# Unread products of zeros in TensorE's planned waits, and batch 1's V loads, spreads and casts behind batch 0's

## The chip, the core and the metric

The kernel runs on one core of one Trainium2 chip. The core has five engines with a queue each, which run side by side and wait for one another by semaphores: TensorE (PE; matrix products into PSUM), VectorE (DVE), ScalarE (ACT), GpSimd (POOL) and SyncE (SP). The queues of SP, ACT and POOL issue DMAs, which 16 DMA engines carry out. The instructions of each engine are brought from HBM by DMA as well. The metric is the device time of one execution in microseconds; lower is better.

## The reference

Two stages, one behind the other: attention with local and global tokens, then a hard-swish MLP over all tokens.

```python
k_all = np.concatenate([k_g, k_l], axis=2)
v_all = np.concatenate([v_g, v_l], axis=2)
out_g = np.matmul(sm(scale * q_g @ k_all.T), v_all)
mask = np.abs(pos[:, None] - pos[None, :]) <= 32
s_ll = np.where(mask, scale * q_l @ k_l.T, -1e9)
out_l = np.matmul(sm(np.concatenate([scale * q_l @ k_g.T, s_ll], -1)), v_all)
x = concat([out_g, out_l], axis=2) as tokens x 512
h = x @ w_in
out = (h * np.clip(h + 3.0, 0.0, 6.0) / 6.0) @ w_out
```

8 batches, 8 heads of 64, 512 local and 32 global tokens a batch, w_in 512 x 2048, w_out 2048 x 512. In the kernel products run in 16 bit with sums in 32 bit.

## The kernel before

Tokens of a batch are cut into 16 blocks of 32 queries; each sees 128 keys: its own block, the block on each side and the 32 global ones. Two blocks from each half of the sequence are a *pair* in what follows: `local` (L697) runs four of them a batch, with 64 score products of TensorE (L731 for batches 0 and 1, L718 for later ones), eight maxima of VectorE (L762), eight exponentials of ScalarE (L768), eight transposes of TensorE (L777), a copy out of PSUM (`et`, L319/L321), 32 products with V (L795), a division (L804, L805) and a transpose into the MLP's layout (L818). Batch 0's pairs run in the order 1, 0, 2, 3; the text counts them first to fourth. `globe` (L822) does the global queries in two halves. The MLP's first product is L926, with ScalarE's relu (L937) and VectorE's gate (L933) behind it; the second is L953. Batch 0's MLP starts pair by pair, with 128 columns for the first two pairs and 256 for the last two.

V is needed in a layout in which the keys of one block stand in the 128 partitions (`vs`). SP's DMAs spread the global rows into it (L532), and copies of *strips* from `v0` (L561) do the rest, on GpSimd for later batches and on any of three engines in batch 0. K and q are turned by VectorE transposes (L609, L614), and at the halves' edges small copies (`halo`, L631) complete K.

The order of all this isn't written by hand. Every operation is put into a named stream with a rank (L297), with its engine or engines, a planned duration and its dependencies. `Plan.lay` (L123) takes, again and again, the operation that can start first by its own clock, and among those that can start within 0.03 us on the same engine the one of lowest rank. It emits them in that order, and the hardware runs each engine's instructions in it. `holds` and a dependency that is added to a plan operation bind the order that is planned. The planner has its own idea of TensorE's instruction supply: blocks of `BLOCK` = 256 instructions, each usable `FETCH` after the edge before it was crossed (`stalls`, L113), and of a slow TensorE (`SLOW`) before `COLD`. None of this appears in the program itself.

At the start TensorE gets a *pad* (L1015): 100 products of a 32x32 tile of zeros with two columns, which nobody reads.

Lines that matter below: `g_first` and `once` load batch 0's and 1's global q and k rows and cast them (L461, L486), `v_loads` (L536) issues V's loads and the strips, `vg_load` and `spread` (L517, L526) the global rows of V, `load_w_in` and `load_w_out` the weights.

Of the kernel before, what the change touches and what calls it, by code (L numbers as in the profile page):

```python
# [9 lines left out]
FP32 = mybir.dt.float32  # L10
# [27 lines left out]
class Plan:  # L38
# [2 lines left out]

    LANES = 8
    BLOCK = 256
    FETCH = 3.4
    COLD, SLOW = 30.0, 1.9
    SWITCH, ALONE = 0.097, 0.0
    SPARE, PHASES = 0.4, 9

    def __init__(self, pools, claims):
        self.count, self.fetched, self.mode = 60, 0.0, "full"  # L50
        self.claims = claims
        self.tune = TUNE
        self.issued = {}
        self.free = {p: [0.0] * n for p, n in pools.items()}
        self.streams = {}
        self.rank = {}
# [66 lines left out]
    def lay(self):  # L123
        at = self.at = {n: 0 for n in self.streams}
        clock = {}
        order = []
        total = sum(len(s) for s in self.streams.values())
        while len(order) < total:
# [43 lines left out]
            at[n] += 1  # L172
            if op.landing is not None:
                self.issued.setdefault(e, []).append(op.landing)
            if e == "PE":
                wait, when = self.stalls(op, start, self.cost(op, e, start))
                end += wait
                self.mode = op.mode[1]
                if self.count % self.BLOCK + op.n >= self.BLOCK:
                    self.fetched = when + wait + self.FETCH + min(3.0, max(0.0, clock.get("DMA", 0.0) - when - 0.5))  # L180
                self.count += op.n
            clock[e] = end
            op.end, op.engine = end + op.lat, e
# [10 lines left out]
def kernel(  # L194
# [52 lines left out]
    def tiles(name, n, shape, dtype, pool=None):  # L247
        return [(pool or sb).tile(shape, dtype, tag=f"{name}{i}", name=f"{name}{i}") for i in range(n)]
# [88 lines left out]
    def quarter(e, f):  # L337
        return slice((2 * e + f) * W, (2 * e + f + 1) * W)
# [121 lines left out]

    def g_first(b):  # L461

        after = [w_in_l[1][1]] if b else []
        state[b]["gl"] = {}
        for k, src, name in ((1, k_g, "k"), (0, q_g, "q")):
            if b == 0:
                once(k, src, name)
                continue
            rows = src[b].rearrange("(c e) g d -> e g c d", e=2)
            g, w, got = Buf("gn" + name, 1), Buf("gr" + name, 1), []  # L470
            state[b]["gn", k] = g
            for e in range(2):
                for f in range(2):
                    got.append(load("sh" if b else "ga" if k else "g0", "SP" if b or not k else "ACT", 0.47, 0.2, graw[k][quarter(e, f)], rows[e], after, () if got else [w]))

            def cast(engine, k=k):
                o, i = (t[k].rearrange("p c d -> p (c d)") for t in (gn0, graw))
                if engine == "ACT":
                    nc.scalar.copy(out=o, in_=i)
                else:  # L480
                    nc.vector.tensor_copy(out=o, in_=i)
            op = Op({"ACT": 0.37, "DVE": 0.3}, None, got, [g], [w])
            op.emit = lambda op=op, cast=cast: cast(op.engine)
            state[b]["gl"][k] = [plan.add("gc", op)]

    def once(k, src, name):  # L486

        raw_ = ots[k][0:W].rearrange("g (h d) -> g h d", d=D)
        got = load("ga", "ACT", 0.47, 0.3, raw_, src[0].rearrange("h g d -> g h d"))
        state[0]["gn", k] = Buf("gn" + name, 1)  # L490
        state[0]["gl"][k] = []
        for e in range(2):
            for f in range(2):
                def cast(engine, e=e, f=f):
                    o, i = gn0[k][quarter(e, f)], raw_.rearrange("g (c e) d -> g e c d", e=2)[:, e]
                    if engine == "ACT":
                        nc.scalar.copy(out=o, in_=i)
                    else:
                        nc.vector.tensor_copy(out=o, in_=i)
                op = Op({"ACT": 0.37, "DVE": 0.3} if k else {"ACT": 0.37}, None, [got], [state[0]["gn", k]] if not state[0]["gl"][k] else [])  # L500
                op.emit = lambda op=op, cast=cast: cast(op.engine)
                state[0]["gl"][k].append(plan.add("gc" if k else "gd", op))

    def g_rest(b0, to):

# [20 lines left out]
    def spread(b, units_, after):  # L526

        st = state[b]
        v = st["v"]
        for u in units_:  # L530
            a = ORDER[u].index("g") * W
            st["vs"][u, 0] = [load("sh", "SP", 0.5, 0.3, lambda u=u, a=a: vs[v.slot][a:a + W, u],  # L532
                                lambda: vg[v.slot][0:W].rearrange("p (j h) d -> p j h d", j=1).to_broadcast([W, NJ, H, D1]), [after], lat=2.0 + LATE[b])]
            st["vs"][u, 1] = list(st["vs"][u, 0])

    def v_loads(b, to):  # L536
# [6 lines left out]
        vl = [load(to, "POOL", 0.8, 1.05 if b else 1.25, lambda j=j: v0[v.slot][:, j, :, 0:D],  # L543
                   v_l[b, :, j * P:(j + 1) * P, :].rearrange("h s d -> s h d"), lat=LATE[b] if b else 3.3 - 0.4 * j) for j in range(NJ)]
# [467 lines left out]

    with tc.manual_schedule():
        clean = plan.add("first", Op(("DVE", 0.1), lambda: nc.vector.memset(zero, 0.0)))
        plan.add("pad", Op(("PE", 4.0), lambda: [nc.tensor.matmul(out=aps[0][0:W, 0, 0:2], lhsT=zero, rhs=zero[:, 0:2], start=True, stop=True) for _ in range(100)], [clean],  # L1015
                           n=200, mode=("small", "small")))
# [79 lines left out]
```

## Time and profile before

| | us |
|---|---|
| median of 3 runs (330.26 to 330.88) | 330.26 |
| the profiled execution | 331.21 |
| its span, first to last instruction | 329.4 |
| TensorE busy, of the span | 306.1 (93%) |
| VectorE busy | 259.6 (79%) |
| ScalarE busy | 236.7 (72%) |
| GpSimd busy | 154.7 (47%) |

The profile shows one execution. "Busy" is the time in which an engine executes; an instruction that waits isn't busy. A line of a wait names who waited, then who ended the wait ("issue": nothing that the profile shows), the total, how often and the longest. A line in order of time has start and length in us, the engine, the line of the kernel, the operation, output and inputs by the program's names, shape and count, and in brackets the idle time before it. PEld is TensorE's weight load. PEclk is TensorE's clock as granted, as a share of full speed; where there is no record yet, it is shown as full.

The largest groups of TensorE are L953 (560 products, 131.8 us) and L926 (640, 121.6 us); of VectorE L933 (136, 92.0 us) and L762 (56.2 us); of GpSimd L561 (87 strips, 79.4 us).

### The profile page before, as it was taken

To read this page: it belongs to the slowest core of one execution; us is meant where nothing else is said; L and a number is where in the kernel's file an instruction comes from. 1 tells how busy PE (TensorE), PEld (TensorE's weight loads), DVE (VectorE), ACT (ScalarE), POOL (GpSimd) and SP (SyncE) were. 2 spreads that over 40 slices of the span, in tenths; PEclk is the share of its full clock that TensorE was granted. 3 is DMA by queue.
4 is the path that set the end of the run, shared out by engine and by line. 5 is a ranking of instruction groups with operands and counts; after the bars stand their busy time and mean duration, and the time that the engine had idled before them with its cause. 6 is when DMAs were issued, how large, how long until landed. Compare 5 with 4: busy or idle time off the path is not lost.

```text
span 329.4 us, 11223 instructions
## 1 busy us (share of the span) xinstructions
PE 306.1 (93%) x4484; PEld 172.8 (52%) x4484; DVE 259.6 (79%) x916; ACT 236.7 (72%) x545; POOL 154.7 (47%) x201
## 2 busy tenths in 40 slices
PE   4457889999989999999999999999999999999995
PEld 3336786555545555555554554554455545556653
DVE  7789996898878898989899899898898874672210
ACT  7869668757977798769867987589758796553221
POOL 9998299409995802993249519923800000000000
PEclk9977999999999999999999999999999999999999
DMA  8999999999952996299969991998211012101222
GB/s 199 186 207 193 206 210 113 176 251 162 191 106 66 157 178 124 47 134 180 211 88 147 169 131 34 120 190 145 62 39 34 2 34 67 32 2 33 65 57 72
DMA packets 105429, 39.67 MB, mean 120 GB/s; under 512 B 92256, under 2 KB 98144, under 8 KB 105376
## 3 DMA queue, kind: packets, MB, share of 16 engines
q0 software_dynamic: 91392, 16.91, 65.8%
q1 hardware_dynamic: 13440, 21.91, 28.2%
q8 instruction: 35, 0.57, 0.7%
q10 hardware_dynamic: 544, 0.13, 0.2%
q14 instruction: 18, 0.15, 0.1%
HBM read 35.26 MB, written 8.91 MB: 134 GB/s over the span
## 4 chain that ended last, share of the span: by engine, by line
PE 76%; POOL 9%; issue 6%; DVE 4%; ACT 2%; DMA 1%; SPq 0%; POOLq 0%
PE m L953 32%; PE m L926 31%; PE t L777 3%; POOL vs L561 3%; PE a L795 3%; PE s L718 2%; POOL v L309 2%; DMA rawq<-rawq 1%; PE s L835 1%; PE t L866 1%; PE a L876 1%; DVE gts L933 1%; PE s L731 1%; DVE x L805 1%; PE m L731 1%
## 5 line engine op out<-in xcount | busy, mean ns | idle before, releaser
L953 PE MATMUL m<-wout,gts 128*128 128x512 f16 (+1 forms) x560 | 131.8, 373 | 0.0
L926 PE MATMUL m<-xt,win 128*128 128x512 f16 (+2 forms) x640 | 121.6, 339 | 3.3 <-DVE gts L933 3.3
L933 DVE SCALAR_TENSOR_TENSOR gts<-t,m 128x512 f16<-128x512 f32 x136 | 92.0, 681 | 30.5 <-ACT t L937 29.0
L937 ACT ACTIVATE t<-m 128x512 f32<-128x512 f32 x136 | 80.8, 596 | 43.4 <-PE m L926 41.2
L561 POOL COPY vs<-v 32x1056 f32<-32x1056 f32 (+5 forms) x87 | 79.4, 912 | 48.9 <-DMA v<-in_v_l_dram 44.8
L926 PEld LDWEIGHTS <-win 128*128 128x128 f16 x704 | 70.7, 114 | 49.6 <-issue 4.9
L768 ACT ACTIVATE ex<-sm,mx 128x128 f16<-128x128 f32 x256 | 86.3, 395 | 10.1 <-DVE mx L762 9.5
L953 PEld LDWEIGHTS <-gts 128*128 128x128 f16 x560 | 51.2, 98 | 49.8 <-issue 2.4
L762 DVE CUSTOM_DVE_ANT_0 sm<-s,mask 128x128 f32<-128x128 f32 x240 | 56.2, 284 | 8.1 <-PE s L731 3.2
L961 ACT COPY ot<-m 128x512 f32<-128x512 f32 (+1 forms) x35 | 20.0, 572 | 12.6 <-PE m L953 12.6
L319 ACT COPY et<-t 128x1024 f16<-128x1024 f16 x26 | 26.2, 1006 | 3.3 <-PE t L777 3.1
L309 POOL DMA_DIRECT2D v<-in_v_l_dram x32 | 28.2, 900 | 0.0
L309 POOL DMA_DIRECT2D rawq<-in_q_l_dram x12 | 12.6, 1056 | 23.9 <-DVE qt L665 13.0
L805 DVE TENSOR_TENSOR x<-a,rec 128x512 f16<-128x512 f32 x32 | 22.1, 692 | 1.1
L818 DVE STREAM_TRANSPOSE xt<-x 128x512 f16<-128x512 f16 x32 | 22.4, 701 | 0.2
L762 DVE DVE_READ_ACCUMULATOR2_ANT mx<- 128x1 f32 x256 | 21.2, 83 | 0.0
L777 PEld LDWEIGHTS <-ex 128*128 128x128 f16 x256 | 17.4, 102 | 6.3 <-issue 0.4
L777 PE MATMUL t<-ident,ex 128*128 128x128 f16 x240 | 19.2, 225 | 0.0
L795 PEld LDWEIGHTS <-et 128*32 128x32 f16 x1024 | 10.0, 97 | 14.1 <-ACT ex L768 3.8
L665 DVE STREAM_TRANSPOSE qt<-rawq 128x512 f16<-128x512 f16 x24 | 15.8, 687 | 0.6 <-DMA rawq<-rawq 0.6
L795 PE MATMUL a<-vs,et 128*32 128x65 f16 x1024 | 14.2, 196 | 2.0 <-ACT et L319 1.1
L319 ACT COPY etg<-t 128x640 f16<-128x640 f16 x15 | 10.4, 693 | 7.6 <-PE t L866 7.5
(93 smaller groups left out, 220.4 us busy)
## 6 DMA issues: line engine op xcount, KB each, us to landing
out_dram<-ot SPq DMA_DIRECT2D x62, 128.0 KB, 2.4
vs<-vg SPq DMA_DIRECT2D x32, 132.0 KB, 7.6
v<-in_v_l_dram POOLq DMA_DIRECT2D x32, 128.0 KB, 9.1
rawq<-in_q_l_dram POOLq DMA_DIRECT2D x12, 256.0 KB, 5.8
rawk<-in_k_l_dram POOLq DMA_DIRECT2D x12, 256.0 KB, 7.6
rawq<-rawq SPq DMA_DIRECT2D x12, 254.0 KB, 7.1
rawk<-rawk SPq DMA_DIRECT2D x12, 254.0 KB, 7.5
win<-in_moe_w_in_dram POOLq DMA_DIRECT2D x4, 512.0 KB, 10.3
```

The lines of the kernel that those rows point to most:

```text
L309: eng.dma_start(out=o() if callable(o) else o, in_=i() if callable(i) else i)
L319: nc.scalar.copy(out=o(), in_=i())
L561: (nc.gpsimd if op.engine == "POOL" else nc.vector).tensor_copy(out=o(), in_=i())
L762: nc.vector.tensor_tensor_reduce(out=sms[sm.slot], in0=scored(c // 2)[:, z:z + P], in1=mask(m), scale=-scale, scalar=3.0e38, op0=ALU.add, ...
L768: nc.scalar.activation(out=exs[ex.slot][:, un, c, :], in_=sms[sm.slot], func=EXP, scale=-1.0, bias=mxs[mx.slot])
L777: nc.tensor.matmul(out=turned(tp)[:, z:z + P], lhsT=exs[ex.slot][:, un, c, :], rhs=ident, is_transpose=True)
L795: nc.tensor.matmul(out=o[hq * W:(hq + 1) * W, 4 * f + 2 * un + kh, 0:D + 1], lhsT=ets[et.slot][:, un, c, quarter(e, f) if b >= WORDS else ...
L805: nc.vector.tensor_tensor(out=xs[x.slot].rearrange("p g (a d) -> p g a d", a=2), in0=o[:, :, 0:D].rearrange("p g (d a) -> p g a d", a=2), ...
L926: nc.tensor.matmul(out=mps[ps.slot][:, k * n:(k + 1) * n], lhsT=column_tile(c)[:, m], rhs=x, start=(m == 0), stop=(m == KC - 1))
L933: nc.vector.scalar_tensor_tensor(out=g, in0=shape(t1s[t1.slot][:, 0:all_]), scalar=1.0, in1=shape(mps[ps.slot][:, 0:all_]), op0=ALU.min, o ...
L937: r = plan.add("t1", Op(("ACT", 0.09 + all_ * 0.00083), lambda: nc.scalar.activation(out=t1s[t1.slot][:, 0:all_], in_=mps[ps.slot][:, 0:al ...
L953: nc.tensor.matmul(out=mps[ps.slot][:, 0:n], lhsT=gfn(c), rhs=w_out_t[c // 4][:, c % 4, cols], start=(c == 0), stop=(c == NDFF - 1))
```

## The change

The planner's numbers change: `COLD` 30 to 16 us, `SPARE` 0.4 to 0.8 (what an operation that could also run on ScalarE must save to be put on VectorE), the supply of instructions 7.0 us a block before 40 us and 5.2 after, and many ranks. Wherever the planner's own TensorE clock has a gap of over 0.4 us between 6 and 60 us, it now puts in products of zeros with zeros, which fill 65% of the gap at a planned 0.057 us each. They write 62 columns at the end of a PSUM tile in which the products with V leave these columns unused. 40 of the pad's 100 products become such full products. Batch 1's global rows are loaded once, in two DMAs rather than eight, and cast by eight smaller copies on ScalarE or GpSimd. In the plan's order, batch 1's global V load on GpSimd comes behind batch 0's last strip, and batch 1's spreads behind the third load of w_out.

```diff
-    FETCH = 3.4
-    COLD, SLOW = 30.0, 1.9
-    SWITCH, ALONE = 0.097, 0.0
-    SPARE, PHASES = 0.4, 9
+    COLD, SLOW = 16.0, 1.9
+    SWITCH, ALONE = 0.097, 0.5
+    GAP, SHARE, FILL = 0.4, 0.65, (6.0, 60.0)
+    SPARE, PHASES = 0.8, 9
...
+            gap = start - clock.get("PE", 0.0)
+            if e == "PE" and self.fill and self.GAP < gap and self.FILL[0] < start < self.FILL[1]:
+                n = int(self.SHARE * gap / 0.057)
+                filler = Op(("PE", gap), lambda n=n: self.fill(n), n=2 * n)
+                filler.end, filler.engine = start, "PE"
+                order.append((clock["PE"], "fill", filler))
+                total += 1
+                self.count += filler.n
+                self.mode = "full"
...
-                    self.fetched = when + wait + self.FETCH + min(3.0, max(0.0, clock.get("DMA", 0.0) - when - 0.5))
+                    self.fetched = when + wait + (7.0 if when < 40.0 else 5.2)
...
-    graw = tiles("graw", 2, [P, NC, D], FP32)
+    graw0 = tiles("graw0_", 1, [W, 2, H, D], FP32)[0]
...
-    zero = tiles("zero", 1, [W, W], FP16)[0]
+    zero = tiles("zero", 1, [P, P], FP16)[0]
...
-    for name, rank in (("l0", 0), ("ld", 5), ("lq", -2), ("sh", 0), ("sq", 0), ("st", 2), ("g0", 0), ("ga", -9), ("first", -9), ("pad", -30), ("gc", -6), ("gd", 3), ("cast", -5), ("msk", lambda n: 1 if n < 9 else 1.25), ("tq", lambda n: 0 if n < 8 else 3), ("kg", -1), ("vs", 2.2), ("clr", 1),
-                       ("s", 0.5), ("mx", lambda n: 1.2 if n < 33 else 2.7), ("ex", 1.2), ("t", -0.5), ("etc", 0), ("av", -0.7), ("nm", 1.5),
-                       ("xp", -0.5), ("gx", 1),
-                       ("mf", lambda n: 9 + n * 1e-3), ("ms", lambda n: 9 + (n + len(PARTS) * NDFF + 2) * 1e-3), ("t1", 0), ("gate", -0.7), ("ot", 0)):
+    for name, rank in (("l0", 0), ("ld", 5), ("lq", -2), ("sh", 0), ("sq", 0), ("st", 2), ("g0", 0), ("ga", -9), ("first", -9), ("pad", -30), ("gc", -6), ("gd", 3), ("gp", 3.9), ("cast", -5), ("msk", lambda n: 1 if n < 9 else 1.25), ("tq", lambda n: 1.5 if n < 8 else 4.5), ("kg", 0.5), ("vs", 2.2), ("clr", 1),
+                       ("s", 0.5), ("mx", lambda n: 1.2 if n < 33 else 2.7), ("ex", 0.5), ("t", 1), ("etc", 0), ("av", -0.7), ("nm", 0),
...
+    def once(b, k, src, name):
+        raw_ = (graw0[:, k] if b else ots[k][0:W].rearrange("g (h d) -> g h d", d=D))
+        got = load("sh" if b else "ga", "SP" if b else "ACT", 0.47, 0.45 if b else 0.3, raw_, src[b].rearrange("h g d -> g h d"), [w_in_l[1][1]] if b else ())
...
+                op = Op({"POOL": 0.43, "ACT": 0.42} if b else {"ACT": 0.42, "DVE": 0.4} if k else {"ACT": 0.42}, None, [got], [] if e or f else [g])
...
-            op = Op({"POOL": c, "ACT": c, "DVE": c if n == W else 1.35 * c} if b == 0 else {"POOL": c}, None, [vl[j + dj] for j in js])
+            op = Op({"POOL": 0.25 + 0.205 * len(js), "ACT": 0.2 + 0.22 * len(js), "DVE": c if n == W else 1.35 * c} if b == 0 else {"POOL": c}, None, [vl[j + dj] for j in js])
...
+        def unread(n):
+            for _ in range(n):
+                nc.tensor.matmul(out=aps[0][:, 1, 512 - 62:], lhsT=zero, rhs=zero[:, 0:62], start=True, stop=True)
+        def pad():
+            for _ in range(60):
+                nc.tensor.matmul(out=aps[0][0:W, 1, 512 - 62:512 - 60], lhsT=zero[0:W, 0:W], rhs=zero[0:W, 0:2], start=True, stop=True)
+            unread(40)
+        plan.add("pad", Op(("PE", 3.3), pad, [clean], n=200, mode=("small", "full")))
+        plan.fill = unread
...
+        for u in range(NU):
+            state[1]["vs"][u, 0][0].deps[0].deps.append(w_out_l[NDFF // 2])
...
+        state[1]["g4"].deps[0].holds = {"POOL": made["strips"][-1][1]}
```

In the order that is built, TensorE has 4,625 products rather than 4,484, each with its weight load.

More of the change, by code (lines that the diff above doesn't have):

```diff
@@ L52, in __init__ @@
         self.tune = TUNE
-        self.issued = {}
+        self.issued, self.fill = {}, None
         self.free = {p: [0.0] * n for p, n in pools.items()}
@@ L296 @@
     plan = Plan(sizes, {})
[L297 to L300 removed]
+    for name, rank in (("l0", 0), ("ld", 5), ("lq", -2), ("sh", 0), ("sq", 0), ("st", 2), ("g0", 0), ("ga", -9), ("first", -9), ("pad", -30), ("gc", -6), ("gd", 3), ("gp", 3.9), ("cast", -5), ("msk", lambda n: 1 if n < 9 else 1.25), ("tq", lambda n: 1.5 if n < 8 else 4.5), ("kg", 0.5), ("vs", 2.2), ("clr", 1),
+                       ("s", 0.5), ("mx", lambda n: 1.2 if n < 33 else 2.7), ("ex", 0.5), ("t", 1), ("etc", 0), ("av", -0.7), ("nm", 0),
+                       ("xp", 1), ("gx", 1),
+                       ("mf", lambda n: 9 + n * 1e-3), ("ms", lambda n: 9 + (n + len(PARTS) * NDFF + 2) * 1e-3), ("t1", 0), ("gate", -1.4), ("ot", 0)):
         plan.stream(name, rank)
@@ L461, in g_first @@
     def g_first(b):
-        after = [w_in_l[1][1]] if b else []
         state[b]["gl"] = {}
         for k, src, name in ((1, k_g, "k"), (0, q_g, "q")):
[L466 to L491, printed above, removed]
+            once(b, k, src, name)
+    def once(b, k, src, name):
+        raw_ = (graw0[:, k] if b else ots[k][0:W].rearrange("g (h d) -> g h d", d=D))
+        got = load("sh" if b else "ga", "SP" if b else "ACT", 0.47, 0.45 if b else 0.3, raw_, src[b].rearrange("h g d -> g h d"), [w_in_l[1][1]] if b else ())
+        g = Buf("gn" + name, 1)
+        state[b]["gn", k] = g
+        state[b]["gl"][k] = []
         for e in range(2):
@@ L498, in cast @@
                     else:
-                        nc.vector.tensor_copy(out=o, in_=i)
-                op = Op({"ACT": 0.37, "DVE": 0.3} if k else {"ACT": 0.37}, None, [got], [state[0]["gn", k]] if not state[0]["gl"][k] else [])
+                        (nc.gpsimd if engine == "POOL" else nc.vector).tensor_copy(out=o, in_=i)
+                op = Op({"POOL": 0.43, "ACT": 0.42} if b else {"ACT": 0.42, "DVE": 0.4} if k else {"ACT": 0.42}, None, [got], [] if e or f else [g])
                 op.emit = lambda op=op, cast=cast: cast(op.engine)
-                state[0]["gl"][k].append(plan.add("gc" if k else "gd", op))
+                state[b]["gl"][k].append(plan.add("gp" if b else "gc" if k else "gd", op))
     def g_rest(b0, to):
@@ L531, in spread @@
             a = ORDER[u].index("g") * W
-            st["vs"][u, 0] = [load("sh", "SP", 0.5, 0.3, lambda u=u, a=a: vs[v.slot][a:a + W, u],
+            st["vs"][u, 0] = [load("sh", "SP", 0.5, 0.45, lambda u=u, a=a: vs[v.slot][a:a + W, u],
                                 lambda: vg[v.slot][0:W].rearrange("p (j h) d -> p j h d", j=1).to_broadcast([W, NJ, H, D1]), [after], lat=2.0 + LATE[b])]
@@ L542, in v_loads @@
             made["ident"] = plan.add("clr", Op(("POOL", 0.55), lambda: make_identity(nc, ident)))
-        vl = [load(to, "POOL", 0.8, 1.05 if b else 1.25, lambda j=j: v0[v.slot][:, j, :, 0:D],
+        vl = [load(to, "POOL", 0.88, 1.05 if b else 1.25, lambda j=j: v0[v.slot][:, j, :, 0:D],
                    v_l[b, :, j * P:(j + 1) * P, :].rearrange("h s d -> s h d"), lat=LATE[b] if b else 3.3 - 0.4 * j) for j in range(NJ)]
@@ L1014 @@
         clean = plan.add("first", Op(("DVE", 0.1), lambda: nc.vector.memset(zero, 0.0)))
-        plan.add("pad", Op(("PE", 4.0), lambda: [nc.tensor.matmul(out=aps[0][0:W, 0, 0:2], lhsT=zero, rhs=zero[:, 0:2], start=True, stop=True) for _ in range(100)], [clean],
-                           n=200, mode=("small", "small")))
+        def unread(n):
[7 more added lines that the diff above has]
+        plan.fill = unread
         plan.add("first", Op(("DVE", 3.4), setup))
```

## The prediction, on record before the result was known

> **What bounds the kernel now.** I read the 40 slices first, then TensorE's waits in the first 60 us, then the order of time around the longest of them. The slices:
>
> ```profile
> PE   4457889999989999999999999999999999999995
> DVE  7789996898878898989899899898898874672210
> PEclk9977999999999999999999999999999999999999
> DMA  8999999999952996299969991998211012101222
> ```
>
> A slice is 8.2 us. From the sixth on TensorE is full, so the end is set by when that state is reached and by the work that is left then. After 60 us it idles 0.8, 0.6 and, at the end, 4.0 us (20.00 less 19.16, 40.00 less 39.44, 29.40 less 25.36 in the busy times by stretch). The rest of its 23.2 us of idle time (329.4 less 306.15), some 17.8, is in the start. TensorE's waits from 0 to 60 us (total, times, longest):
>
> ```profile
> PE s L731 <- DVE kt L624: 3.6, 1, 3.6
> PE m L731 <- issue: 3.5, 1, 3.5
> PE s L731 <- DVE kt L614: 3.3, 2, 2.5
> PE m L926 <- DVE gts L933: 3.3, 3, 1.6
> PE m L731 <- POOL kt L631: 1.6, 1, 1.6
> ```
>
> Four name a producer. The 3.5 us of "issue" has none. In order of time, TensorE and then VectorE:
>
> ```profile
> 18.55 0.35 PE L731 MATMUL m<-kt,qt 32*32 32x128 f16 x19
> 22.39 0.83 PE L731 MATMUL m<-kt,qt 32*32 32x128 f16 x45 [3.50 <-issue]
> 23.15 1.03 PE L777 MATMUL m<-ident,ex 128*128 128x128 f16 x8
> 50.72 0.61 PE L777 MATMUL t<-ident,ex 128*128 128x128 f16 x8
> ```
>
> ```profile
> 21.13 0.69 DVE L805 TENSOR_TENSOR x<-a,rec 128x512 f16<-128x512 f32 x1
> 23.33 0.29 DVE L762 CUSTOM_DVE_ANT_0 sm<-m,mask 128x128 f32<-128x128 f32 x1 [1.51 <-PE m L731]
> ```
>
> TensorE stops inside one group of 64 equal products, so no operand is missing: its instructions are. The page's queue table says what brings them:
>
> ```profile
> q8 instruction: 35, 0.57, 0.7%
> ```
>
> 35 packets of 16 KB for a stream of 8,988 instructions are 64 B each, 256 to a packet. At the stop 706 had been issued; with 62 of a preamble that is 768, the third edge of 256. The packets' starts in the trace fit this: 5.43, 20.12, 26.33, 33.08, 39.16 us, behind the first edges' crossings at 3.5, 15.6, 22.4, 28.6 and 35.4 by 1.9, 4.5, 3.9, 4.4 and 3.8. So crossing one edge asks for the block behind the next one. The block that stopped TensorE was asked for at 15.6, came from 20.12 to 21.12 and was usable at 22.39: 6.8 us. With the lags of 3.8 to 4.5, 1.0 for the packet and 1.3 until use, a block takes 6.1 to 6.8 us while the DMA engines are full. In that time TensorE gets 128 products, whatever they are.
>
> The stop costs VectorE only the 1.51 us shown, for it had work queued. VectorE then carries the start (busy, in stretches, behind the arrow of each row's PE and PEld):
>
> ```profile
> 21.33:28.15 6.82, 5.26 (x123) 4.24 (x123) 5.11 (x24) 4.28 (x12) 6.64 (x10) 0.50 1.17 202
> 28.15:42.16 14.01, 10.30 (x256) 8.92 (x254) 13.62 (x25) 10.12 (x22) 5.81 (x11) 1.00 1.48 202
> 42.16:60.00 17.84, 17.58 (x396) 12.91 (x395) 14.11 (x73) 14.57 (x39) 17.35 (x20) 1.00 1.53 162
> ```
>
> 13.62 of 14.01 us is VectorE; from 42.16 TensorE has 17.58 of 17.84. The first row also has the clock at 0.50. The eight transposes took 1.03 us there and 0.61 at full clock.
>
> **The change part by part.** *The unread products.* 100 stand in the pad as before, 40 of them now full tiles; 141 more stand in ten groups: 13, 24, 23, 10, 5, 7, 5, 14, 24 and 16. Their form is not in the trace. From below the pad's 28 ns (2.82 us over 100), from above the 111 ns of a half-clock 128x128 product (1.77 us over 16 at 26.68). I take 62/128 of the latter, 53 ns, as they stream 62 columns; 141 are 7.5 us (3.9 to 15.7). In time they are mostly covered: the 24 and 23 lie in the idle stretches before 10.50 and 11.88 (2.53 and 0.77 us in the trace), 24 behind the third pair's values under ScalarE's exponentials, the last 16 under VectorE's 2.06 us of L614 transposes. Three groups first wait until VectorE has read the same PSUM tile (L805 twice, L893 once); behind them queue the second pair's transposes, the fourth pair's (their exponentials come later still) and products that need a gate behind L614. Without that cover the 24 would cost 1.3 us.
>
> *What they should bring.* Full clock from early on is worth half of TensorE's cold work on the chain: transposes 0.4 us a pair, scores 0.3 (64 in about 1.0 us at 16.8, 0.7 at 44.4), so up to 1.5 us for pairs one and two, and nothing where VectorE is the bound. I take 0.5.
>
> By the Trainium skill (TensorE: Matmul & The Clock Gate, Part 1) a busy window of about 3.4 us gives full clock and one idle window takes it away. The trace agrees: 1.00 granted for 3.4 us from 17.91, 0.50 for 6.8, then 1.00. By it alone the whole 1.5 us would be kept.
>
> *What they take.* 282 instructions are 1.1 blocks, and they come where blocks are scarce. The built order puts the edges so. The second falls on the last of the first pair's third set of scores, which waits for L614 at about 12.7 us (12.3 in the trace; two maxima now stand before it, two times 0.21). The third falls on the 41st of 64 scores of the third pair; those can start near 16.6 (15.87 plus 1.0 in the trace). Its block is usable at 12.7 plus 6.1 to 6.8, 18.8 to 19.5, where before all 64 scores, the first values and 19 products more were done by 18.9. The fourth falls inside the five unread products just ahead of the second pair's transposes. Between the two edges TensorE has 23 scores, 7 unread, 32 values, 64 scores: about 2 us. It then waits to 19.2 plus 6.1 to 6.8, 25.3 to 26.0, and the transposes start at 25.8, against 23.15. Evacuation 1.0 us (24.22 in the trace, 1.01), values 0.5 and the division 0.9 put x of the second pair's end at 28.7 to 29.6, against 27.57. Fifth edge, inside the third pair's values: 31.4 to 32.8, against 28.4 for these values.
>
> From there the fourth pair's chain (transposes, 1.0 us of copy, 20 MoE products, values, 0.9 of division) ends at 37 to 38.4, against 33.8. VectorE comes to batch 1's L609 at 38.1 to 39.7, against 35.02: 3.1 to 4.7 late, with one gate (0.66) and its product group (1.0 us of TensorE) more behind it. Subtracting the 1.0, TensorE is full 2.1 to 3.7 us later.
>
> *VectorE's share.* Two maxima before L614 rather than behind it, a copy etg (0.45) and two strips (0.43, 0.74) to ScalarE or GpSimd: 1.6 us less for VectorE, of which I count 0.5, since in the new order it waits, not TensorE for it. Bound 0 to 1.6.
>
> *Batch 1's V, spreads and casts.* GpSimd takes four strip copies (0.65 each, 2.65 us for four at 21.15) ahead of V's loads, which then go out at about 28 rather than 24.5; behind them w_out's. The values of batch 1 run at 57.9, the loads landed at 37.6, so 3 to 4 us is covered. Without cover it would be 3.5. SP issues two loads of batch 1's global rows rather than eight, ahead of the four spreads in either kernel; nothing there waits. Eight casts of 32x256 (0.40 each, ScalarE five, GpSimd three) replace two of 0.41: 1.2 us more on ScalarE, in its 1.53 us of waiting at 37.
>
> *The ranks* move instructions of all batches, but the groups of TensorE's modes stay as they are (67 returns to full tiles before, 68 after), and TensorE is full: 0, between minus 1.0 and plus 1.0 (the 1.4 us of idle time, or as much again).
>
> **Sum** against the profiled execution, 331.21 us (span 329.4 and 1.8 around it): plus 2.9 (mid of 2.1 to 3.7), minus 0.5 and 0.5 gives plus 1.9, 333.1. The runs' median is 0.95 lower: 332.2.
>
> **Rivals.** *The blocks come in time.* The first lag was 1.9 us, with few small packets under way. With it a block takes 4.2 us; the third edge would be served at 16.9, the fourth at 21.1, just as they are reached. Then the 3.5 us are gone: the second pair's exponentials are done near 20, transposes, copy, values and division (0.5, 1.0, 0.5, 0.9, and some queueing on ScalarE) put its x at 24.3, VectorE's 7.9 us of work from there to L609 at 32.2 rather than 35.0, and the end at 330.26 less 2.8, 327.5. For it: the DMA engines' later lag of 2.4 at 43.1. Against: four of the five lags from 15 to 36 us are near 4, and the engines are full until 54.
>
> The Trainium skill (Runtime: NRT & Kernel Launch, Instruction fetch mechanics) has blocks of 256 instructions with crossings "mostly hidden"; by that this rival holds. The block size agrees with the trace, the 3.50 us stop does not.
>
> *The clock falls in the wait before the fourth edge.* 4 us without products, then half clock: transposes and MoE products of pairs two to four take 1.5 to 2 us more on the chain: 334.0. For it: after 18.90 to 22.39 the clock was 0.50 for 6.8 us. Against: part of it lies under VectorE.
>
> *It comes to nothing:* the stalls eat just the gain of clock and order, 330.3.
>
> **How the numbers follow.** Two stalls as forecast 0.48 (own range 331.0 to 333.6), blocks in time 0.28 (327.0 to 329.5), clock falling as well 0.16, nothing 0.08. Within 0.2%, 0.7 us either way, cannot be told from no change. Faster 0.28; same 0.10, with 0.02 of the forecast's low edge; slower 0.62. The range runs from just past the fast case's middle to just past the clock case: 327.3 to 334.4.
>
> **What would show it.** Right: waits of TensorE by "issue" of about 2 us near 17 to 19 and about 4 near 21 to 26, the second pair's L777 behind the second; L609 of batch 1 after 37. Wrong: no "issue" wait over 1 us before 40, packets of the instruction queue less than 3 us behind the edges, full clock from below 15 us on without a break, or TensorE full before 42.

## The result and the profile after

| | before | after |
|---|---|---|
| median, us (lowest to highest, five runs each) | 330.26 (328.99 to 330.88) | 334.07 (332.38 to 334.87) |
| the profiled execution, us | 331.21 | 334.15 |
| its span, us | 329.4 | 332.3 |
| TensorE busy, us | 306.1 | 313.2 |
| VectorE busy, us | 259.6 | 254.5 |

The changed kernel is slower: ratio of its times to those of before 1.0092, 95% interval 1.0065 to 1.0119. That is 3.0 us, between 2.1 and 3.9; the two medians differ by 3.81. The four slices of before stand in the prediction; these are three of after:

```profile
PE   6747889999999999999999999999999999999995
DVE  6775798689968998989998999889989875432210
PEclk9556999999999999999999999999999999999999
```

TensorE is busier in the first two slices (the unread products) and, as before, full only from the seventh on (the prediction said the sixth, whose digit is an 8). The clock is at half in slices 2 and 3: exactly, the windows give 1.00 for 3.4 us from 6.03, 0.50 for 20.5 us from 9.45, and 1.00 from 29.93.

Where the time went is read off one identity. The last wait of the start is that of a group of 256-column MLP products for a gate (before L926, 42.16 us; after L917, 46.83). From there on:

```profile
46.83:332.30 285.47, 280.78 (x3750) 151.85 (x3749) 220.38 (x776) 206.71 (x463) 123.09 (x132) 1.00 0.87 105
```

285.47 us are left after it, of which TensorE works 280.78. Before, 287.24 were left. So TensorE is full 4.67 us later, and 1.77 us less is left then (0.76 of it work, 281.54 less 280.78, the rest idle time); the difference is the 2.9 us between the spans. What makes the kernel slower lies ahead of 46.83. (In after each line number of before is some 9 lower: scores L722, transposes L768, values L786, x L796, turns L600 and L605; L1009 are the unread products of 62 columns.) The six longest of TensorE's waits there (total, times, longest):

```profile
PE a L1009 <- issue: 3.7, 1, 3.7
PE a L1009 <- DVE x L796: 2.3, 1, 2.3
PE s L722 <- DVE kt L615: 1.9, 1, 1.9
PE s L722 <- DVE kt L605: 1.5, 1, 1.5
PE m L917 <- DVE gts L924: 1.5, 2, 0.8
PE s L722 <- issue: 1.1, 1, 1.1
```

The one stop without a producer (3.50 us before) has become two, 1.12 and 3.66, and the unread products themselves wait for VectorE. In order of time:

```profile
17.20 0.73 PE L722 MATMUL s<-kt,qt 32*32 32x128 f16 x40
19.05 0.52 PE L722 MATMUL s<-kt,qt 32*32 32x128 f16 x24 [1.12 <-issue]
...
21.64 0.21 PE L1009 MATMUL a<-zero 128*128 128x62 f16 x1
25.52 0.36 PE L1009 MATMUL a<-zero 128*128 128x62 f16 x4 [3.66 <-issue]
25.70 1.04 PE L768 MATMUL m<-ident,ex 128*128 128x128 f16 x8
...
31.65 0.42 PE L786 MATMUL a<-vs,et 128*32 128x65 f16 x32
34.36 0.84 PE L1009 MATMUL a<-zero 128*128 128x62 f16 x24 [2.29 <-DVE x L796]
35.03 0.61 PE L768 MATMUL t<-ident,ex 128*128 128x128 f16 x8
```

Both stops lie inside groups of equal products. Counted in the trace, 351 products and 352 weight loads had started before the first, 479 and 480 before the second: 703 and 959 instructions, 256 apart. Before's one stop stands at 703 too. The second pair's transposes start at 25.70, against 23.15. VectorE and ScalarE were drawn in:

```profile
28.12 0.29 DVE L753 CUSTOM_DVE_ANT_0 sm<-m,mask 128x128 f32<-128x128 f32 x1 [4.45 <-ACT ex L759]
```

```profile
26.77 1.01 ACT L328 COPY et<-m 128x1024 f16<-128x1024 f16 x1 [5.71 <-PE m L768]
```

ScalarE waits 5.71 us for those transposes, the exponentials behind that copy wait with it, and VectorE, whose maxima write the tiles that these exponentials read, stops for 4.45 us. Before it had stopped for 1.51.

### The profile page after: what moved, and what is told of

It is laid out like the page before. It is cut to its first block, busy times and chain, and to the rows that moved or that the text cites. A ratio compares the mean times of both kernels' runs of the same rounds, so it can differ in the third digit from the quotient of the medians.

```text
span 332.3 us, 11483 instructions
## 1 busy us (share of the span) xinstructions
PE 313.2 (94%) x4625; PEld 180.0 (54%) x4625; DVE 254.5 (77%) x908; ACT 241.4 (73%) x555; POOL 157.1 (47%) x205
## 4 chain that ended last, share of the span: by engine, by line
PE 82%; DVE 8%; POOL 4%; ACT 3%; issue 2%; POOLq 0%; ACTq 0%; DVEq 0%
PE m L944 34%; PE m L917 32%; PE t L768 4%; PE a L786 3%; PE s L709 3%; DVE gts L924 2%; DVE sm L753 2%; PE t L857 1%; ACT ex L759 1%; PE s L826 1%; POOL v L318 1%; ACT et L328 1%; PE a L867 1%; DVE x L796 1%; POOL win L318 1%
## 5 line engine op out<-in xcount | busy, mean ns | idle before, releaser
L917 PE MATMUL m<-xt,win 128*128 128x512 f16 (+2 forms) x640 | 123.1, 339 | 1.7 <-DVE gts L924 1.5
L552 POOL COPY vs<-v 32x1056 f32<-32x1056 f32 (+5 forms) x90 | 81.1, 901 | 36.4 <-DMA v<-in_v_l_dram 32.1
L917 PEld LDWEIGHTS <-win 128*128 128x128 f16 x704 | 70.6, 115 | 47.4 <-issue 3.7
L759 ACT ACTIVATE ex<-sm,mx 128x128 f16<-128x128 f32 x256 | 85.0, 396 | 5.6 <-DVE mx L753 4.8
L328 ACT COPY et<-t 128x1024 f16<-128x1024 f16 x31 | 31.2, 1006 | 5.7 <-PE t L768 5.6
L796 DVE TENSOR_TENSOR x<-a,rec 128x512 f16<-128x512 f32 x32 | 22.1, 692 | 1.1
L768 PEld LDWEIGHTS <-ex 128*128 128x128 f16 x256 | 17.3, 101 | 6.2 <-ACT ex L759 0.2
L768 PE MATMUL t<-ident,ex 128*128 128x128 f16 x248 | 19.4, 222 | 0.0
L786 PEld LDWEIGHTS <-et 128*32 128x32 f16 x1024 | 10.1, 98 | 12.0 <-issue 3.4
L660 DVE STREAM_TRANSPOSE kt<-rawk 128x512 f16<-128x512 f16 x24 | 15.7, 682 | 0.0
```

Source lines behind the costliest of these rows:

```text
L759: nc.scalar.activation(out=exs[ex.slot][:, un, c, :], in_=sms[sm.slot], func=EXP, scale=-1.0, bias=mxs[mx.slot])
L768: nc.tensor.matmul(out=turned(tp)[:, z:z + P], lhsT=exs[ex.slot][:, un, c, :], rhs=ident, is_transpose=True)
L796: nc.vector.tensor_tensor(out=xs[x.slot].rearrange("p g (a d) -> p g a d", a=2), in0=o[:, :, 0:D].rearrange("p g (d a) -> p g a d", a=2), ...
L917: nc.tensor.matmul(out=mps[ps.slot][:, k * n:(k + 1) * n], lhsT=column_tile(c)[:, m], rhs=x, start=(m == 0), stop=(m == KC - 1))
```

## The experiments

Unread products and the pad can be left out, resized or added without a change in what is computed; the two bindings only order work. So every kernel below computes all of the outputs. Ratios are to before, on the same chip. The kernels were run in four sets, in which before's median was 330.26, 330.63, 330.15 and 330.62 us, so medians of different sets compare less well than ratios.

**The change without its unread products; without its two bindings.**

```diff
-        plan.fill = unread
+        plan.fill = lambda n: None
```

> The changed kernel with its planned order, but none of the 141 unread products emitted (the pad keeps its 60 and 40). Instruction supply (my theory): the second edge falls on the 59th product of the second pair's scores again, at about 15.5 us, the third at 20 products of the fourth pair's scores, usable near 22.2; one stop of about 3 us, the second pair's transposes near 23.2 rather than 25.7, TensorE full some 3 us earlier than with the products: 329.5 to 331. Order (rival: the ranks, holds and casts cost the time): 333 to 335, as the changed kernel. Clock (rival: the products are needed for the clock): slower than the changed kernel, over 334.5.

Measured: 330.59 us (330.16 to 332.22, ten runs), ratio 1.0003 (0.998 to 1.0026). One stop is left, 2.19 us, and the same work stands behind the same last wait as in after:

```profile
43.30:328.80 285.50, 280.92 (x3750) 151.71 (x3749) 220.35 (x776) 206.48 (x463) 122.93 (x132) 1.00 0.87 108
```

So the unread products cost 3.5 us by the medians (334.07 less 330.59) and by the profiles (46.83 less 43.30), 2.9 by the ratios; all the rest of the change, new order, fewer copies on VectorE, bindings and casts, is worth nothing that can be measured (the interval allows 0.7 us less to 0.9 more). 3.29 of the 3.5 have come by the second pair's transposes (22.41 here, 25.70 in after).

```diff
-        for u in range(NU):
-            state[1]["vs"][u, 0][0].deps[0].deps.append(w_out_l[NDFF // 2])
...
-        state[1]["g4"].deps[0].holds = {"POOL": made["strips"][-1][1]}
```

> The changed kernel without its two bindings of batch 1's V loads and spreads behind batch 0's strips and w_out. Instruction supply: third and fourth edge stand where they are in the changed kernel, with stops to 19.1 and 25.5: 333 to 335. Holds (rival: later V loads cost the time): 331 to 332.5.

Measured: 335.2 us (334.28 to 336.22, four runs), ratio 1.0133 (1.0092 to 1.0175). The stop ahead of the second pair's transposes stays (3.44 us, up to 24.44). The plan came out otherwise, though: it has 155 unread products rather than 141, a group of 30 behind MLP products instead of the 24 behind the third pair's values, and two later stops (0.60 and 0.48 us). So this run only shows that the kernel isn't faster without the bindings; that they are not what costs is shown by the run above it, which has them.

**Time of the products, or their number?** First, a quarter as many products, each over four times the columns (248):

```diff
...
+        def wide(n):
+            for _ in range((n + 3) // 4):
+                nc.tensor.matmul(out=aps[0][:, 1].rearrange("p (g d) -> p g d", g=4)[:, :, P - 62:], lhsT=zero,
+                                 rhs=zero[:, 0:62].rearrange("p (j d) -> p j d", j=1).to_broadcast([P, 4, 62]), start=True, stop=True)
+        plan.fill = wide
```

> The changed kernel with the same planned order, but each unread product four times as wide (248 columns) and a quarter as many of them: 39 for 141, the same TensorE time, a quarter of the instructions. Instruction supply: second edge in the second pair's scores near 15.3, third among the first pair's values, fourth at the end of the second pair's values; no stop ahead of the second pair's transposes: 329.5 to 331. Time of the products themselves, or their waits for VectorE (rival): 333 to 335. Clock: if full clock early is worth anything, it is under e1_no_fill by up to 1.5 us.

Measured: 335.49 us (332.58 to 336.55, four runs), ratio 1.0127 (1.0069 to 1.0186). A miss, and no clean test: with fewer instructions the edges moved, into the values of the first and of the second pair (stops of 2.66 and 2.14 us), and the group behind the third pair's values waited 1.90 us (2.29 in after). So next the edges were kept and the time changed. Same 141 products, same places, but each a 32x32 tile with 2 columns:

```diff
...
+        def small(n):
+            for _ in range(n):
+                nc.tensor.matmul(out=aps[0][0:W, 1, 512 - 62:512 - 60], lhsT=zero[0:W, 0:W], rhs=zero[0:W, 0:2], start=True, stop=True)
+        plan.fill = small
```

> After with the same 141 unread products in the same places, but each a 32x32 tile of zeros with 2 columns (about 28 ns in the pad's rows, against 55 to 60). The number of instructions, and so every edge of 256, is as in after; TensorE's own time for the products is halved. Theory (the products cost by the instructions they use up): 333 to 334.5 us, with stops of TensorE by issue of about 1 us at 19 and 3 to 4 us up to 25 to 25.6 and the second pair's transposes at about 25 to 26. Rival (the products cost by TensorE's time or by what they do to the clock): 331 to 332.

Measured: 335.67 us (332.74 to 335.89, four runs), ratio 1.0131 (1.0091 to 1.0172), over both ranges. The stops, which are what the run was to test:

```profile
19.06 0.52 PE L722 MATMUL s<-kt,qt 32*32 32x128 f16 x24 [1.39 <-issue]
...
25.80 0.24 PE L1019 MATMUL a<-zero 32*32 32x2 f16 x4 [4.05 <-issue]
25.98 1.03 PE L768 MATMUL m<-ident,ex 128*128 128x128 f16 x8
```

The products are over sooner (the 23 take 0.79 us where 62 columns took 1.37), TensorE reaches both edges at the same instructions, waits longer, and the transposes start where they did (25.98, 25.70). Nearly halving the products' time brings nothing; their number sets the stops. (The runs of the two kernels overlap; what the profile of this one loses against after, it loses behind this point, by the clock, below.)

The other way round, many columns in few instructions, with the edges put where less waits (a pad of 75) and without the group behind the third pair's values:

```diff
-            for _ in range(60):
+            for _ in range(35):
...
+            for _ in range((n + 3) // 4 if len(groups) != 9 else 0):
```

> After with about a quarter as many unread products, of 248 columns each, none behind the third pair's values, and a pad of 75 (35 small, 40 of 62 columns), so that the third edge falls in the fourth pair's scores and no edge inside the first or second pair's values. Nearly the same columns of zeros stream as in after, with some 110 instructions pairs fewer. Theory (supply): one stop of 2 to 3.5 us up to about 22 to 22.5, second pair's transposes at 22.5 to 23, 330 to 331.5. Rival (the time that the products stream costs by itself): 332.5 or more.

Measured: 331.19 us (330.28 to 331.75, ten runs), ratio 1.0012 (0.9988 to 1.0035), with one stop:

```profile
15.83 0.61 PE L768 MATMUL t<-ident,ex 128*128 128x128 f16 x8
...
22.47 0.82 PE L722 MATMUL m<-kt,qt 32*32 32x128 f16 x43 [3.69 <-issue]
```

33 products still stream the columns of 132, and by the ratios 0.12% is left of 0.92%, 2.6 of 3.0 us gone. Three things were changed here, number, edges and the missing ninth group (below), so the run doesn't say which brought how much. The line at 15.83 says one thing more: the first pair's transposes ran at full clock (0.61 us, 1.04 in after), and the kernel is still no faster than before. What the early clock saved ended in the wait for the block, which lets TensorE go on at 22.47; a kernel without that wait but with the early clock was not run.

Then after with 50 small products more in the pad, which only shifts the edges:

```diff
-            for _ in range(60):
+            for _ in range(110):
```

> After with 50 more small products in the pad (150 rather than 100), which changes nothing but which instruction stands on each edge: second edge in the third set of scores at about 12, third in the unread products ahead of the first pair's transposes at about 16, fourth in the fourth pair's scores, its block usable at about 22.3. Theory (supply): more work and yet faster than after by 0.7 to 1.5, 332.5 to 333.4; second pair's transposes at 23.4 to 24. Rival (products cost by themselves, or removing a stop is covered): 334 or more.

Measured: 335.05 us (334.16 to 336.56, four runs), ratio 1.0131 (1.009 to 1.0173). A miss in the time. The step it was to test came out: one long stop less ahead of the second pair (0.15 and 3.27 us are left), and its transposes at 23.74, 2.0 us sooner than in after. Then this:

```profile
28.72 1.04 PE L917 MATMUL m<-xt,win 128*128 128x128 f16 x8 [1.50 <-issue]
29.55 1.06 PE L768 MATMUL t<-ident,ex 128*128 128x128 f16 x8
...
34.68 0.86 PE L1009 MATMUL a<-zero 128*128 128x62 f16 x24 [1.89 <-DVE x L796]
35.35 1.04 PE L768 MATMUL t<-ident,ex 128*128 128x128 f16 x8
```

The next edge falls into MLP products that stand ahead of the third pair's transposes, and these start at 29.55 (29.82 in after): the 2.0 us are given back to the next block. One stop that is removed early is worth only what the next edge leaves of it. That TensorE is full 1.8 us later than in after (48.63, 46.83) comes behind this point, from the clock (below).

**The unread products alone, in before's order.** Before with the planner's filling (94 products in its gaps) and the changed pad:

```diff
...
+                n = int(self.SHARE * gap / 0.057)
+                filler = Op(("PE", gap), lambda n=n: self.fill(n), n=2 * n)
...
+        plan.fill = unread
```

> The kernel before with the unread products alone (94 of them in its own planned gaps, the changed pad), all its other numbers and ranks kept. Instruction supply: second edge at about 12.9 us behind the third scores, the third at the 52nd of 64 scores of the third pair, usable near 19.2, the fourth behind the second pair's transposes, in the global scores, usable near 25.5: the transposes come at about 21, the second pair's values near 25.7 as before; 329.5 to 331.5. Unread products cost by themselves (rival): 333 or more. They help (rival): under 329.5.

Measured: 333.38 us (333.11 to 335.76, six runs), ratio 1.0093 (1.006 to 1.0125). The time is what the rival had said, but the trace shows stops, not the products' time: 1.25, 2.69, 1.23 and 1.73 us by "issue", at 19.07, 25.26, 38.24 and 52.74. I had placed the edges where less waited. With 94 products 1.0093 and with 141 products 1.0092: the loss does not go with their number alone; in these traces it goes with what stands at the edges that the number moves.

**The position of the edges alone.** Three kernels change nothing but the pad at the start. After without its pad:

```diff
-        plan.add("pad", Op(("PE", 3.3), pad, [clean], n=200, mode=("small", "full")))
+        plan.add("pad", Op(("PE", 3.3), lambda: None, [clean], n=200, mode=("small", "full")))
```

> The changed kernel without the pad's 100 products (its 141 others stay): less work for TensorE, all of it taken out of a stretch in which it idles. Instruction supply: the first edge now falls behind the first pair's third scores, near 13.2 us rather than 4.4, so the second block of the stream that must be brought is asked for 9 us later; stops at the 12th of the third pair's scores until 19.4 to 20, and inside the fourth pair's scores until 25.9 to 26.5, the second pair's transposes near 26.8 (25.7 in the changed kernel), the third pair's values over 1 us later: 335 to 336.5, slower than the changed kernel by 0.5 to 2. Products' own time, or order (rivals): no change or faster, 333 to 334.3.

Measured: 332.78 us (331.92 to 334.13, four runs), ratio 1.0085 (1.0058 to 1.0111). A miss: I had misread where the edges fall: the first is crossed at 11.68, the second at 17.27 without a stop, and the next block was usable 6.17 us after that, at 23.44, in the fourth pair's scores, and the second pair's transposes came at 24.23, 1.5 us sooner than in after. The time is no slower than after, as the rival had it; the trace is of the slowest run (334.13).

Before without its pad, and before with a pad of 166 products instead of 100:

```diff
-        plan.add("pad", Op(("PE", 4.0), lambda: [nc.tensor.matmul(out=aps[0][0:W, 0, 0:2], lhsT=zero, rhs=zero[:, 0:2], start=True, stop=True) for _ in range(100)], [clean],
+        plan.add("pad", Op(("PE", 4.0), lambda: [nc.tensor.matmul(out=aps[0][0:W, 0, 0:2], lhsT=zero, rhs=zero[:, 0:2], start=True, stop=True) for _ in range(166)], [clean],
```

> The kernel before without its 100 unread products at the start, nothing else changed; TensorE idles there anyway. Instruction supply: the first edge moves from 3.5 us into the second pair's scores, near 15.2, the next block is usable at 21.4 to 22 and TensorE stops at the 23rd of the first pair's values (reached near 18.5), then at the last of the second pair's values until about 28: 331 to 333, slower than before. Otherwise (rival: the pad does nothing): 330.0 to 330.9.

> The kernel before with 166 rather than 100 unread products at the start (1.8 us more in a stretch of idle time), nothing else changed. Instruction supply: the second edge falls near the end of the first pair's scores at about 12.3 us, so that the third block is usable at 18.5 to 19 (22.4 before) and the fourth, in the global scores, at 24.8 to 25.5; the second pair's transposes come near 20.8 rather than 23.15, its values near 25.5 as before, VectorE's 1.5 us of waiting goes: 328.5 to 330.2, faster than before by up to 1.5. Otherwise (rival): 330.0 to 331.5.

Without the pad: 332.06 us (331.79 to 332.5, four runs), ratio 1.0064 (1.0046 to 1.0081). The kernel has 100 useless products less and is about 2 us slower, since the first edge is crossed not at 3.5 but at 15.20, and the two after it stop the values of two pairs:

```profile
21.34 0.25 PE L795 MATMUL a<-vs,et 128*32 128x65 f16 x9 [2.64 <-issue]
...
27.45 0.23 PE L795 MATMUL a<-vs,et 128*32 128x65 f16 x1 [2.41 <-issue]
```

With 166: 332.71 us (331.03 to 333.12, six runs), ratio 1.0069 (1.0048 to 1.0089), a miss. Before's 3.50 us stop is gone (0.16 is left) and the second pair's transposes start at 21.86 instead of 23.15. But TensorE then waits where it didn't before: 1.74 us for the spread of V's global rows, 0.94 for ScalarE's exponentials and 0.64 at a later edge (up to 36.87), and the last wait of the start ends at 41.95, against 42.16. So the stop had lain over other waits. In its profile (331.03) nothing is lost; why most of the other runs took some 1.6 us more stays open.

The same pad in the change without unread products, as a try at a version that beats both:

```diff
-            for _ in range(60):
+            for _ in range(126):
...
+        plan.fill = lambda n: None
```

> After's order without the 141 unread products, and with a pad of 166 (126 small, 40 of 62 columns) so that no edge is reached ahead of its block in the start. The attempt at a version that beats both. Theory: the 2.2 us stop of the kernel without fills goes, the second pair's transposes start near 21, its x ends 1.3 earlier, 329 to 330.5. Rival (a stop of 2 us here is covered by the spreads' landing and by ScalarE, as before with a pad of 166): 330 to 332.5.

Measured: 332.2 us (330.37 to 334.31, twelve runs), ratio 1.0049 (1.0026 to 1.0071). A miss, within the rival's range. The transposes came at 20.38, as foreseen, but the next edge fell into the global scores ahead of the second pair's values (1.71 us, up to 24.69). The last wait of the start ends at 43.52, 0.2 later than without the longer pad, and 286.7 us are left after it rather than 285.5: further on other edges are hit, one of them 0.67 us at 131.47, in a later batch, which is part of it. A shift of the stream moves every edge behind it. No kernel here is measurably faster than before.

**The group behind the third pair's values.** After without the ninth group, the 24 products that wait 2.29 us for VectorE:

```diff
-        plan.fill = unread
+        groups = []
...
+        def all_but_ninth(n):
+            groups.append(n)
+            if len(groups) != 9:
+                unread(n)
+        plan.fill = all_but_ninth
```

> The changed kernel without its ninth group, the 24 products behind the third pair's values whose first waits until VectorE has divided these values. If this wait holds up the fourth pair's transposes: they start near 33.9, as soon as their exponentials are there, rather than 35.03, and the time is about 1 us under the changed kernel, 332.7 to 333.7. If the group is covered, as the prediction had it: no change, 333.7 to 335.

Measured: 333.02 us (332.69 to 333.17, four runs), ratio 1.0087 (1.0072 to 1.0102). From the third pair's x to the fourth's (starts of L796) it is 3.88 us here and 4.63 in after (33.61 to 38.24), 0.75 us less. In after, the fourth pair's last exponentials and the third x end like this:

```profile
32.46 1.56 ACT L759 ACTIVATE ex<-sm,mx 128x128 f16<-128x128 f32 x5
33.61 0.69 DVE L796 TENSOR_TENSOR x<-a,rec 128x512 f16<-128x512 f32 x1
```

The exponentials are done at 34.02, the x at 34.30; the 24 products wait for the x, and the transposes stand behind them until 35.03. Without the group the transposes start as the exponentials come, two at 31.18 and six at 32.38. The times alone don't tell the two kernels apart: 1.05 us by the medians, 0.2 by the ratios, whose intervals overlap.

**All together.** By the trace of each kernel, start of the second pair's transposes, third to fourth x, start of the 256-column group, and the rest from there to the end of the span, us; the last column is the median of all runs:

| kernel | transposes | x to x | group | rest | median |
|---|---|---|---|---|---|
| change, no unread products | 22.41 | 4.14 | 43.30 | 285.5 | 330.59 |
| 248 columns, pad 75 | 23.61 | 3.81 | 44.17 | 285.1 | 331.19 |
| no unread products, pad 166 | 20.38 | 3.93 | 43.52 | 286.7 | 332.20 |
| no ninth group | 24.91 | 3.88 | 45.26 | 285.9 | 333.02 |
| no pad | 24.23 | 6.12 | 46.86 | 285.4 | 332.78 |
| after | 25.70 | 4.63 | 46.83 | 285.5 | 334.07 |
| 248 columns | 23.28 | 6.09 | 48.35 | 285.6 | 335.49 |
| pad 150 | 23.74 | 6.12 | 48.63 | 285.5 | 335.05 |
| 2 columns | 25.98 | 6.12 | 48.97 | 285.1 | 335.67 |

In four of the five kernels that have the ninth group the step from x to x is 6.1 rather than 4.6. These are two stretches of the one with 2 columns:

```profile
30.00:35.80 5.80, 3.91 (x88) 3.76 (x86) 5.36 (x15) 4.89 (x13) 5.65 (x10) 0.99 1.88 164
35.80:39.20 3.40, 3.40 (x43) 2.74 (x44) 0.91 (x2) 2.12 (x4) 0.32 (x1) 0.51 1.06 208
```

After the wait for the third x the clock is 0.51 for 3.4 us, and TensorE, fully busy in it, is what the chain waits for. In after it stayed at 1.00. So the ninth group costs 0.75 us by its wait, and some 1.5 more where the clock falls.

Why it falls in four kernels and not in after can be read off the clock's records. In every trace the clock switches 3.41 us or a multiple of it apart (in after at 6.03, 9.45 and 29.93), so one can count stretches of 3.41 us from the switches. In the four kernels the wait for the third x lies whole within one stretch, of which TensorE works 1.3 to 1.5 us, and the next is at 0.50. This is the kernel without pad, whose stretch runs from 29.99 to 33.40:

```profile
30.00:33.40 3.40, 1.31 (x59) 1.20 (x57) 3.30 (x7) 2.96 (x10) 3.31 (x6) 1.00 1.99 170
33.40:36.80 3.40, 3.40 (x51) 2.74 (x48) 0.93 (x2) 2.10 (x4) 2.51 (x5) 0.50 1.68 192
```

In after a boundary at 33.35 cuts the wait in two; TensorE works 2.1 and 2.4 us in the two stretches, and the clock stays. Counted so, up to 60 us in all fourteen traces, a stretch at full clock with at most 1.65 us of work was followed by half clock, and one with 1.69 or more was not. By the Trainium skill (TensorE: Matmul & The Clock Gate, Part 1) the windows run freely and the cold count varies from run to run. The traces agree as far as they go: counted back by 3.41 us to the start of the span, the first boundary lies at 2.6 us in after, at 1.6 with 2 columns and at 1.0 with 248. That the boundaries also lie otherwise from run to run of one kernel would fit the spread of their times (331.92 to 334.13 without pad), but only one run of each has a trace.

## Why the prediction was right, and where it was off

It said 332.2 us, slower; measured were 334.07. That is above the 331.0 to 333.6 that it gave to two stalls as forecast, and within its whole range only because this reaches past the clock rival's 334.0. Direction and mechanism were right; that the range held the number is in part luck.

- *The supply of instructions:* right, step by step. Second edge crossed at 12.7, measured 12.93; third block usable 18.8 to 19.5, 19.05; fourth 25.3 to 26.0, 25.52; transposes 25.8, 25.70; fifth edge inside the third pair's values at 31.4 to 32.8, 31.75, without a stop. The count of 706 instructions at before's stop is 703 in the trace, and the preamble of 62 was fitted to that stop; but in all fourteen traces each stop by "issue" up to 30 us stands at 447, 703, 959 or 1,215 started instructions, to within one, so the edges were put right. That number, not time, makes the stops is shown by the 2-column kernel.
- *From there to full TensorE:* the second x ended at 30.17 (28.7 to 29.6 forecast), 0.6 beyond, because the division stands behind the maxima of the stopped VectorE and a strip; the counterpart of L609 came at 40.07 (38.1 to 39.7), 5.05 us late where 3.1 to 4.7 was forecast, 0.75 of it from the ninth group. Net TensorE was full 4.67 less 1.77, 2.9 us later, the middle of 2.1 to 3.7; but 1.0 had been subtracted and not 1.77, so that two errors cancel in it.
- *The ninth group "covered":* wrong. "Their exponentials come later still" failed: these ended at 34.02, the third x at 34.30 and the 24 products behind it. Without cover it was to cost 1.3; 0.75 were measured in the trace.
- *Minus 0.5 for the clock:* did not come. The early full clock (6.03 to 9.45) lay where TensorE waits for VectorE's turns, and the full clock for good came 1.8 us later than before (29.93, 28.15). The prediction's reading that it takes an idle window to lose it was too mild: before's stretch from 17.91 had 0.71 us of work, and with 1.3 to 1.65 us it was lost in others. Nor did it show in the time where the first pair's transposes did get it (the kernel with 248 columns and a pad of 75, 1.0012).
- *Minus 0.5 for VectorE's share:* cannot be seen; the change without unread products is at 1.0003, and its interval is just wide enough for 0.5. Batch 1's loads, spreads and casts at nothing, and the ranks at nothing, fit the same run, which has all of them together and tells none from the others.
- *The miss of 1.87 us:* from profiled run to profiled run plus 1.9 was forecast and 2.94 measured (334.15 less 331.21): 1.0 for the two gains that did not show, while the 2.9 for the supply was met. The other 0.9 is the step from the profiled run to the median, 0.95 in before and only 0.08 in after.
- *The rivals:* "blocks in time" fell: no stop up to 30 us ended less than 5.7 us after the edge before it. "The clock falls" gave 334.0, but not for its reason: the clock was at half from 9.45, ahead of both stops, and the kernel without unread products, which costs nothing, is at half until 28.44 too (transposes of 1.03 us at 22.41). Where a wait did pull it down and cost time, it was that for the third x, in other kernels.

The Trainium skill (Runtime: NRT & Kernel Launch, Instruction fetch mechanics) calls the crossing of a block "mostly hidden". From 43.5 us on it is, but for waits of 0.2 to 1.7 us; in the start 13 of the 14 traces have a stop of 1.7 to 4.1 us, and only before with a pad of 166 has none over 0.64.

## What to carry to other kernels

An instruction that does nothing is not free where the instruction stream is late: count instructions to each edge of 256, mark which group stands there, and see who waits behind it, before anything is filled in. Idle time of the engine is not enough: filler takes instructions as well as time. No filler paid here. The cheapest had many columns in few instructions, with its edges placed and without the group behind the third pair's values (1.0012); few instructions alone, without that, cost 1.0127. A pad or a filler moves all later edges, so one early stop that is removed may come back at the next edge, or uncover a wait that it hid.

## What the runs showed of the hardware

- Up to 30 us, with the DMA engines full, a stop ended 5.8 to 6.8 us after the edge before had been crossed (6.0 in the change without unread products, 6.1 and 6.5 in after, 6.5 and 6.7 with 2 columns, 6.8 before), however long or short the products in between were.
- Fewer instructions can be slower: before without its 100 useless products takes about 2 us more (332.06 against 330.15).
- After 3.4 us in which TensorE worked 1.31 us, the next 3.4 us had a clock of 0.50 (the kernel without pad, 30.00 to 33.40 and 33.40 to 36.80), though TensorE was busy for all of the latter. So a stretch need not be idle to cost the clock, while a wait of 2.29 us that a boundary cut in two did not cost it (after).
